# A long convolution and a gated MLP on one core: where the last inverse stage's copy, sum and difference stand in the queues

## The chip, the cores and the metric

The kernel runs on one core of a Trainium2 chip. The metric is the device time of one execution in microseconds (us). The engines are called as the profile calls them: PE (TensorE, matrix products, with PEld for its weight loads), DVE (VectorE), ACT (ScalarE), POOL (GpSimd) and SP (SyncE, which here issues every DMA). Each engine works through its own instructions in the order in which they are written, and waits at an instruction until the others have delivered.

## The reference

Two layers follow each other. The first convolves `x*v` along the sequence (4 batches, 12480 positions, 128 channels) with a filter that a small network makes, and multiplies by `x`; the second is a gated MLP with 2048 inner features.

```python
h_filt = (np.maximum(pos_emb @ w1, 0.0) @ w2) * np.exp(-0.01 * pos)[:, None]
u = x * v
y = irfft(rfft(u, 2*S) * rfft(h_filt, 2*S), 2*S)[:, :S]   # along the sequence
x1 = (x * y).reshape(B * S, D)
h = x1 @ w_in
out = (h * np.clip(h + 3.0, 0.0, 6.0) / 6.0) @ w_out
```

## The kernel before, in words

The transforms are done as two short transforms each, as products with tables on PE. The convolution is cut into eight groups of channels and batches (`NG = 8`), each group into 25 chunks (`NCHUNK`) of four frequencies. The function `period(g)` walks through the chunks of group g and writes, chunk by chunk, work of three groups side by side:

- of group g itself (`chunk`): PE makes the chunk's spectra (`second_stage`, L300). ACT copies their two halves crosswise into another PSUM bank, the swap (`swapped`, L498 and L499; there is one such bank, tag `sw`). DVE multiplies spectra and swapped spectra with the filter's (`products`, L519 to L522). POOL adds the products up in three steps (L526): two small additions, into `a` and into `a2`, and the final sum `a + a2`. Three chunks later PE takes the sum back (`third_stage`, L541) and ACT copies the result into `z` (L545).
- of group g - 1, whose `z` is complete: PE transposes it (`back`, L552), ACT copies the transposes into `w` (L555), and for every fourth of these (one block of 16 columns) the last inverse stage follows (`fourth_stage`): PE multiplies the block with a table into two PSUM banks, `same` and `other` (L569), ACT copies `other` into SBUF (L579), DVE forms sum and difference of `same` and this copy (L581, two instructions), and SP stores the block to `yd` in HBM (L584).
- of group g + 1: POOL multiplies loaded pieces of `x` and `v` (`gate_next`, L452, eight or nine for a group), and eight times for a group PE makes a first stage of four tiles (`visit`, L281), each copied into `z` by ACT (L293).

During the first group, which has no group ahead of it to take back, DVE does the final sum of two chunks in three (L531; chunks whose number is not a multiple of 3), and POOL does the others.

The first stages, `back` and the fourth stage share one set of three PSUM banks (tag `ts`); a new tile takes the bank that was let go first. The spectra share two banks (tag `s2`). In the first groups of those that have a `back`, DVE also decodes the MLP's weights in small steps (L225 to L247), in three stretches for each of five groups and one more.

After the eighth group `last_turn` takes its own `z` back, and then the MLP (class `Moe`) runs for the rest of the time. Nothing is reordered by a scheduler: the order in the code is the order in each engine's queue.

Of the kernel before, what the change touches and what calls it, by code (L numbers as in the profile page):

```python
# [188 lines left out]
def pool(tc, name, bufs=1, **kw):  # L189
    return tc.tile_pool(name=name, bufs=bufs, reuse_waits="tile", **kw)  # L190
# [60 lines left out]
class Conv:  # L251
    def __init__(self, tc, nc, left, right, x, v, c_tab, d_tab, g_tab, ident, hd, yd, weights):
        self.tc, self.nc, self.left, self.right = tc, nc, left, right
        self.x, self.v, self.g_tab, self.ident, self.hd, self.yd = x, v, g_tab, ident, hd, yd
        self.c_tab, self.d_tab, self.weights = c_tab, d_tab, weights
        self.loaded, self.gated, self.n_loaded = [], [], 0
        self.first, self.second, self.pend, self.steps = [], [], [], None
        self.tabs, self.n_tabs, self.hs, self.n_hs = [], 0, [], 0
        self.keep = right.enter_context(pool(tc, "keep", side="right"))
        self.z = [self.keep.tile([128, K2, COLS], F32, name=f"z{i}") for i in range(2)]  # L260
        self.dtab = self.keep.tile([K2, 2, 64], F32, name="dtab")
        big = left.enter_context(pool(tc, "big"))
        self.ctab = big.tile([R[0], 2 * K2], F32, name="ctab")
# [238 lines left out]
    def products(self, item):  # L502

        nc, P = self.nc, 128
        g, c, kw, t, tab = item
        sw = self.swapped(t, kw)
        hs = self.hs.pop(0)
        a = self.pr.tile([P, CH, 2 * GB, G], F32, tag="a", name="pa", bufs=4)
        a2 = self.pr.tile([P, CH, 2 * GB, G], F32, tag="a2", name="pa2")
        q = self.pr.tile([P, CH, GB, G], F32, tag="q", name="pq")  # L510
        q2 = self.pr.tile([P, CH, GB, G], F32, tag="q2", name="pq2")
        uv = t.rearrange("p (k s g) -> p k s g", k=CH, g=G)[:, :kw]
        sv = sw.rearrange("p (k s g) -> p k s g", k=CH, g=G)[:, :kw]

        def h(ci, si, m):
            return hs[:, ci, :kw, si, :].unsqueeze(2).to_broadcast([P, kw, m, G])

        mul, add = ALU.mult, ALU.add
        nc.vector.tensor_tensor(out=q[:, :kw], in0=uv[:, :, :GB], in1=h(0, 1, GB), op=mul)  # L519
        nc.vector.tensor_tensor(out=a[:, :kw], in0=uv, in1=h(0, 0, 2 * GB), op=mul)  # L520
        nc.vector.tensor_tensor(out=q2[:, :kw], in0=sv[:, :, :GB], in1=h(1, 1, GB), op=mul)
        nc.vector.tensor_tensor(out=a2[:, :kw], in0=sv, in1=h(1, 0, 2 * GB), op=mul)  # L522
        self.load_h()

        def plus(x, y):
            nc.gpsimd.tensor_tensor(out=x, in0=x, in1=y, op=add)  # L526

        plus(a[:, :kw, GB:], q[:, :kw])
        plus(a2[:, :kw, GB:], q2[:, :kw])
        if g == 0 and c % 3:  # L530
            nc.vector.tensor_tensor(out=a[:, :kw], in0=a[:, :kw], in1=a2[:, :kw], op=add)  # L531
        else:
            plus(a[:, :kw], a2[:, :kw])
        return g, c, kw, tab, a
# [24 lines left out]
    def fourth_stage(self):  # L559


        if not self.pend:
            return
        nc = self.nc
        g, col, w = self.pend.pop(0)
        same, other = (self.bank("ts") for i in range(2))
        for c, t in enumerate((same, other)):
            for h in range(2):
                nc.tensor.matmul(  # L569
                    t[64 * h : 64 * h + 64, :],  # L570
                    self.dtab[:, c, :],
                    w[:, GH * h : GH * h + GH, c * N1 : (c + 1) * N1],
                    start=True,
                    stop=True,
                )
        y = self.wp.tile([128, 2, N1, GH], F32, tag="y", name="y")
        same, other = (t.rearrange("p (c n) -> p n c", c=GH) for t in (same, other))
        o = self.wp.tile([128, N1, GH], F32, tag="o", name="o", bufs=1)
        nc.scalar.copy(o, other)  # L579
        for i, op in enumerate((ALU.add, ALU.subtract)):  # L580
            nc.vector.tensor_tensor(out=y[:, i], in0=same, in1=o, op=op)  # L581
        piece, ch = divmod(col, G)
        k, b, d = self.place(g, piece)
        nc.sync.dma_start(self.yd[b][k][d // G, ch // GY], y)  # L584
# [29 lines left out]
    def chunk(self, g, c):  # L614

        if g == 0 and c == 0:
            self.first.append(self.spectra(0, 0))
        self.second.append(self.products(self.first.pop(0)))
        lag = LAG if START < c < NCHUNK - 1 else LAG - 1
        self.third_from(lag)  # L620
        g, c = (g, c + 1) if c + 1 < NCHUNK else (g + 1, 0)
        if g < NG:
            self.first.append(self.spectra(g, c))
        self.third_from(lag)
# [26 lines left out]
    def last_turn(self, moe):  # L651

        self.fourth_stage()
        for n, col in enumerate(range(0, COLS, 4)):
            self.back(NG - 1, col)
            if n % 4 == 2:
                self.fourth_stage()
            if n in (10, 12):
                moe.load(n // 2 - 5)
            if n == 20:  # L660
                moe.gate(0)
            if n == 28:
                moe.turn(0)
        self.fourth_stage()


class Moe:
# [208 lines left out]
```

## Time and profile before

| | |
|---|---|
| median of three runs | 3205.4 us (3201.54 to 3206.84) |
| profiled execution, its own time | 3204.68 us |
| its span in the profile | 3202.9 us |
| PE busy | 3125.8 us (98%) |
| DVE busy | 2328.0 us (73%) |
| ACT busy | 2347.2 us (73%) |
| POOL busy | 2078.4 us (65%) |
| PE's granted clock, mean over the span | 0.997 of 2.4 GHz |

The span runs from the first to the last instruction on the engines; 1.8 us of the execution's own time lie around it. The ends of PE's products are modelled, so that a busy PE can still be short of its peak; its idle time is the safer figure. A matrix product of 32-bit numbers shows as two records.

### The profile page before, as it was taken

To read this page: it belongs to the slowest core of one execution; us is meant where nothing else is said; L and a number is where in the kernel's file an instruction comes from. 1 tells how busy PE (TensorE), PEld (TensorE's weight loads), DVE (VectorE), ACT (ScalarE), POOL (GpSimd) and SP (SyncE) were. 2 spreads that over 40 slices of the span, in tenths; PEclk is the share of its full clock that TensorE was granted. 3 is DMA by queue.
4 is the path that set the end of the run, shared out by engine and by line. 5 is a ranking of instruction groups with operands and counts; after the bars stand their busy time and mean duration, and the time that the engine had idled before them with its cause. 6 is when DMAs were issued, how large, how long until landed. Compare 5 with 4: busy or idle time off the path is not lost.

```text
span 3202.9 us, 53380 instructions
## 1 busy us (share of the span) xinstructions
PE 3125.8 (98%) x19916; PEld 2638.1 (82%) x19916; DVE 2328.0 (73%) x2707; ACT 2347.2 (73%) x3039; POOL 2078.4 (65%) x1240
## 2 busy tenths in 40 slices
PE   9978999999999999999999999999999999999999
PEld 8967888888887788888888888888888888888887
DVE  4467677667656577777777777777777777777776
ACT  2346676666677787787777777777777877778777
POOL 1167777777777366666666666666666666666666
PEclk9999999999999999999999999999999999999999
DMA  6667878877765311111111111011011111111110
GB/s 230 211 167 201 238 217 225 226 216 229 215 183 187 117 30 40 40 33 41 33 40 37 33 40 40 30 40 40 30 40 40 30 40 40 33 37 40 36 35 23
DMA packets 232273, 304.66 MB, mean 95 GB/s; under 512 B 38055, under 2 KB 159310, under 8 KB 231118
## 3 DMA queue, kind: packets, MB, share of 16 engines
q1 hardware_dynamic: 232014, 301.26, 32.2%
q8 instruction: 157, 2.57, 0.3%
q14 instruction: 102, 0.84, 0.1%
HBM read 224.87 MB, written 76.28 MB: 94 GB/s over the span
## 4 chain that ended last, share of the span: by engine, by line
PE 67%; POOL 0%; DVE 0%; DMA 0%; ACT 0%; issue 0%; ACTq 0%
PE acc L808 11%; PE acc L804 11%; PE acc L805 11%; PE ph L769 11%; PE ph L771 11%; PE ph L770 11%; PE ts L569 1%; PE s L552 0%; PE ts L552 0%; POOL pa L526 0%; DMA yd<-y 0%; POOL glo L793 0%; DVE y L581 0%; ACT ghi L791 0%; PE s L541 0%; DVE o L821 0%
## 5 line engine op out<-in xcount | busy, mean ns | idle before, releaser
L793 POOL TENSOR_TENSOR glo<-g,ghi 128x1024 fp32r<-128x1024 f32 x588 | 1405.6, 2399 | 759.3 <-ACT ghi L791 759.2
L781 DVE SCALAR_TENSOR_TENSOR g<-r,ph 128x1024 f32<-128x1024 f32 (+1 forms) x784 | 949.5, 1211 | 408.5 <-ACT r L779 408.3
L779 ACT ACTIVATE r<-ph,three 128x1024 f32<-128x1024 f32 (+1 forms) x784 | 871.3, 1111 | 273.7 <-PE ph L771 273.4
L791 ACT CAST ghi<-g 128x1024 fp32r<-128x1024 f32 (+1 forms) x784 | 810.9, 1034 | 1.9 <-DVE g L781 1.0
L769 PE MATMUL ph<-xhi,win_hi 128*128 128x512 f32 (+1 forms) x1568 | 608.5, 388 | 0.0
L770 PE MATMUL ph<-xlo,win_hi 128*128 128x512 f32 (+1 forms) x1568 | 608.4, 388 | 0.0
L771 PE MATMUL ph<-xhi,win_lo 128*128 128x512 f32 (+1 forms) x1568 | 608.3, 388 | 0.0
L805 PE MATMUL acc<-ghi,wout_lo 128*128 128x512 f32 (+1 forms) x1568 | 608.0, 388 | 0.0
L804 PE MATMUL acc<-ghi,wout_hi 128*128 128x512 f32 (+1 forms) x1568 | 607.9, 388 | 0.0
L808 PE MATMUL acc<-glo,wout_hi 128*128 128x512 f32 (+1 forms) x1568 | 481.3, 388 | 0.6 <-POOL glo L793 0.6
L526 POOL TENSOR_TENSOR pa<-pa,pq 128x256 f32<-128x256 f32 (+1 forms) x400 | 291.5, 735 | 209.1 <-DVE pa L520 175.8
L769 PEld LDWEIGHTS ph<-xhi,win_hi 128*128 128x128 f32 x1568 | 294.5, 188 | 61.6 <-issue 0.8
L808 PEld LDWEIGHTS acc<-glo,wout_hi 128*128 128x128 f32 x1568 | 293.5, 188 | 61.9 <-POOL glo L793 1.5
L805 PEld LDWEIGHTS acc<-ghi,wout_lo 128*128 128x128 f32 x1568 | 294.5, 188 | 60.6
L770 PEld LDWEIGHTS ph<-xlo,win_hi 128*128 128x128 f32 x1568 | 294.5, 188 | 60.3
L771 PEld LDWEIGHTS ph<-xhi,win_lo 128*128 128x128 f32 x1568 | 294.3, 188 | 60.6
L804 PEld LDWEIGHTS acc<-ghi,wout_hi 128*128 128x128 f32 x1568 | 294.3, 188 | 60.4
L793 DVE TENSOR_TENSOR glo<-g,ghi 128x1024 fp32r<-128x1024 f32 x196 | 284.2, 1450 | 0.0
L300 PE MATMUL s<-z,tab 128*128 128x128 f32 x1584 | 218.7, 282 | 57.9 <-DVE pa L520 28.3
L742 DVE TENSOR_TENSOR xy<-xt,yt 128x512 f32<-128x512 f32 x96 | 258.5, 2693 | 0.0
L300 PEld LDWEIGHTS s<-z,tab 128*128 128x128 f32 x1584 | 195.3, 194 | 69.3 <-issue 29.4
L526 POOL TENSOR_TENSOR pa<-pa,pa 128x512 f32<-128x512 f32 (+1 forms) x184 | 233.6, 1270 | 14.4
(61 smaller groups left out, 3529.6 us busy)
## 6 DMA issues: line engine op xcount, KB each, us to landing
tab<-in_g_tab SPq DMA_DIRECT2D x192, 256.0 KB
h<-hd SPq DMA_DIRECT2D x384, 128.0 KB
yd<-y SPq DMA_DIRECT2D x64, 512.0 KB
xt<-in_xt SPq DMA_DIRECT2D x98, 256.0 KB
out<-o SPq DMA_DIRECT2D x97, 256.0 KB
xt<-in_x SPq DMA_DIRECT2D x64, 384.0 KB
vt<-in_v SPq DMA_DIRECT2D x64, 384.0 KB
yt<-yd SPq DMA_DIRECT2D x256, 64.0 KB
```

The lines of the kernel that those rows point to most:

```text
L300: self.nc.tensor.matmul(t[:, i * 128 : (i + 1) * 128], tab[:, i, :], z[:, c * CH + i, :], start=True, stop=True)
L526: nc.gpsimd.tensor_tensor(out=x, in0=x, in1=y, op=add)
L769: nc.tensor.matmul(ph[:, i, :ne], self.win_hi[:, sl], hi[:, :ne], start=True, stop=False)
L770: nc.tensor.matmul(ph[:, i, :ne], self.win_hi[:, sl], lo[:, :ne], start=False, stop=False)
L771: nc.tensor.matmul(ph[:, i, :ne], self.win_lo[:, sl], hi[:, :ne], start=False, stop=True)
L779: nc.scalar.activation(r[:, :, :ne], ph[:, :, :ne], AF.Relu, bias=self.three)
L781: nc.vector.scalar_tensor_tensor(out=g[:, :, :ne], in0=r[:, :, :ne], scalar=6.0, in1=ph[:, :, :ne], op0=ALU.min, op1=ALU.mult)
L791: nc.scalar.copy(ghi[:, :, :ne], g[:, :, :ne])
L793: e.tensor_tensor(out=glo[:, :, :ne], in0=g[:, :, :ne], in1=ghi[:, :, :ne].bitcast(F32), op=ALU.subtract)
L804: nc.tensor.matmul(a, self.wout_hi[:, f, :], ghi[:, i, :ne], start=(f == 0), stop=False)
L805: nc.tensor.matmul(a, self.wout_lo[:, f, :], ghi[:, i, :ne], start=False, stop=False)
L808: nc.tensor.matmul(a, self.wout_hi[:, f, :], glo[:, i, :ne], start=False, stop=(f == NFC - 1))
```

## The change

`fourth_stage` is cut in two. It keeps the products on PE, and remembers their two banks; the copy on ACT, the sum and the difference on DVE and the store move into a new function, `results`, which is called behind the next chunk's `products` (or, where a second block would come first, ahead of that block's products on PE). In `last_turn` it is called right behind each fourth stage. And in the first group the final sum that DVE does for a chunk is written one chunk later, behind that chunk's four multiplications.

```diff
+        if self.sum:
+            s, s2 = self.sum
+            nc.vector.tensor_tensor(out=s, in0=s, in1=s2, op=add)
+        self.sum = None
         if g == 0 and c % 3:
-            nc.vector.tensor_tensor(out=a[:, :kw], in0=a[:, :kw], in1=a2[:, :kw], op=add)
+            self.sum = a[:, :kw], a2[:, :kw]
         else:
             plus(a[:, :kw], a2[:, :kw])
...
         if not self.pend:
             return
+        self.results()
         nc = self.nc
         g, col, w = self.pend.pop(0)
...
+        self.out = g, col, same, other
+
+    def results(self):
+
+        if self.out is None:
+            return
+        nc = self.nc
+        g, col, same, other = self.out
+        self.out = None
         y = self.wp.tile([128, 2, N1, GH], F32, tag="y", name="y")
...
         self.second.append(self.products(self.first.pop(0)))
+        self.results()
         lag = LAG if START < c < NCHUNK - 1 else LAG - 1
...
         self.fourth_stage()
+        self.results()
```

No instruction is added or removed. With the two insertions the lines move: what is L498, L499, L519 to L522, L531, L579 and L581 before is L499, L500, L520 to L523, L533, L594 and L596 after.

On DVE in the first group, at the products of chunks 4, 5 and 6 (`pa` is a chunk's `a`, `pa2` its `a2`, `s2` its spectra, `sw` the swap), before:

```order
L522 TENSOR_TENSOR pa2_2148<-sw_2144,h_2004 128x512
L531 TENSOR_TENSOR pa_2147<-pa_2147,pa2_2148 128x512
L519 TENSOR_TENSOR pq_2186<-s2_2169,h_2033 128x256
L520 TENSOR_TENSOR pa_2184<-s2_2169,h_2033 128x512
L521 TENSOR_TENSOR pq2_2187<-sw_2181,h_2033 128x256
L522 TENSOR_TENSOR pa2_2185<-sw_2181,h_2033 128x512
L531 TENSOR_TENSOR pa_2184<-pa_2184,pa2_2185 128x512
L519 TENSOR_TENSOR pq_2216<-s2_2206,h_2055 128x256
```

The same place on DVE after the change:

```order
L523 TENSOR_TENSOR pa2_2148<-sw_2144,h_2004 128x512
L520 TENSOR_TENSOR pq_2185<-s2_2168,h_2033 128x256
L521 TENSOR_TENSOR pa_2183<-s2_2168,h_2033 128x512
L522 TENSOR_TENSOR pq2_2186<-sw_2180,h_2033 128x256
L523 TENSOR_TENSOR pa2_2184<-sw_2180,h_2033 128x512
L533 TENSOR_TENSOR pa_2147<-pa_2147,pa2_2148 128x512
L520 TENSOR_TENSOR pq_2215<-s2_2205,h_2054 128x256
L521 TENSOR_TENSOR pa_2213<-s2_2205,h_2054 128x512
L522 TENSOR_TENSOR pq2_2216<-sw_2210,h_2054 128x256
L523 TENSOR_TENSOR pa2_2214<-sw_2210,h_2054 128x512
L533 TENSOR_TENSOR pa_2183<-pa_2183,pa2_2184 128x512
```

The sum of chunk 4 (`pa_2147`) stood directly behind its own products and now stands behind those of chunk 5; that of chunk 5 stands behind those of chunk 6.

On ACT in the third group (group 2, which takes group 1 back), behind the visit and fourth stage of chunk 3 (`z1` copies are the visit's, `sw` the swap of chunk 4, `o` the copy of `other`), before:

```order
L293 COPY z1_79<-ts_4772 128x99x4
L579 COPY o_4789<-ts_4783 128x512
L498 COPY sw_4794<-s2_4725 64x512
L499 ACTIVATE sw_4794<-s2_4725 64x512
L545 COPY z0_78<-s3_4811 128x512
```

The same place on ACT after the change:

```order
L294 COPY z1_79<-ts_4772 128x99x4
L499 COPY sw_4788<-s2_4725 64x512
L500 ACTIVATE sw_4788<-s2_4725 64x512
L594 COPY o_4806<-ts_4783 128x512
L550 COPY z0_78<-s3_4811 128x512
```

The swap of chunk 4 now stands ahead of the fourth stage's copy; on DVE sum and difference likewise stand behind the products of chunk 4.

On DVE in the same group, behind the products of chunk 18 and at the first steps of the third weight decoding (`dec`), before:

```order
L581 TENSOR_TENSOR y_5694<-ts_5688,o_5695 128x512 x2
L519 TENSOR_TENSOR pq_5712<-s2_5637,h_5444 128x256
L520 TENSOR_TENSOR pa_5710<-s2_5637,h_5444 128x512
L521 TENSOR_TENSOR pq2_5713<-sw_5707,h_5444 128x256
L522 TENSOR_TENSOR pa2_5711<-sw_5707,h_5444 128x512
L225 TENSOR_SCALAR dec_5562<-raw_5560 128x256
```

The same place on DVE after the change:

```order
L520 TENSOR_TENSOR pq_5706<-s2_5637,h_5444 128x256
L521 TENSOR_TENSOR pa_5704<-s2_5637,h_5444 128x512
L522 TENSOR_TENSOR pq2_5707<-sw_5701,h_5444 128x256
L523 TENSOR_TENSOR pa2_5705<-sw_5701,h_5444 128x512
L596 TENSOR_TENSOR y_5718<-ts_5688,o_5719 128x512 x2
L225 TENSOR_SCALAR dec_5562<-raw_5560 128x256
```

Sum and difference of that block now stand between the products of chunk 19 and the decoding. On PE and POOL the order of the instructions is the same in both kernels.

## Rows read from the trace of the kernel before

**Rows 1.** Busy time by stretch: stretch, length, PE, PEld, DVE, ACT, POOL, clock, DMA.

```profile
164.00:265.00 101.00, 77.09 (x886) 71.12 (x886) 73.23 (x112) 51.85 (x102) 65.88 (x65) 0.93 0.69 181
265.00:1034.00 769.00, 728.72 (x7189) 633.38 (x7190) 525.16 (x992) 531.68 (x1016) 585.34 (x574) 1.00 0.75 213
1076.00:3202.00 2126.00, 2121.91 (x9403) 1757.70 (x9401) 1641.21 (x1370) 1686.60 (x1763) 1405.65 (x588) 1.00 0.12 37
```

**Rows 2.** Timeline of DVE, first group: start, length, instruction, [idle before it, what ended it].

```profile
210.56 0.69 DVE L531 TENSOR_TENSOR pa<-pa,pa 128x512 f32<-128x512 f32 x1 [0.84 <-POOL pa L526]
211.17 0.42 DVE L519 TENSOR_TENSOR pq<-s,h 128x256 f32<-128x256 f32 x1
...
212.44 0.68 DVE L522 TENSOR_TENSOR pa<-sw,h 128x512 f32<-128x512 f32 x1
213.96 2.83 DVE L531 TENSOR_TENSOR pa<-pa,pa 128x512 f32<-128x512 f32 x1 [0.84 <-POOL pa L526]
216.71 0.41 DVE L519 TENSOR_TENSOR pq<-s,h 128x256 f32<-128x256 f32 x1
...
219.93 0.42 DVE L519 TENSOR_TENSOR pq<-s,h 128x256 f32<-128x256 f32 x1 [1.28 <-ACT sw L499]
...
223.33 0.42 DVE L519 TENSOR_TENSOR pq<-s,h 128x256 f32<-128x256 f32 x1
```

**Rows 3.** Timeline of POOL, the same stretch.

```profile
213.88 2.36 POOL L452 TENSOR_TENSOR u<-xt,vt 98x1024 f32<-98x1024 f32 x1
...
218.79 0.72 POOL L526 TENSOR_TENSOR pa<-pa,pq 128x256 f32<-128x256 f32 x1 [0.19 <-DVE pa L522]
```

**Rows 4.** All of line 531: durations in ns (least, median, most), first and last start.

```profile
L531 DVE TENSOR_TENSOR pa<-pa,pa x16: 692/1754/2849, 171.8 to 264.8; 128x512 f32<-128x512 f32 x16
```

**Rows 5.** Timeline of ACT, the same stretch of the first group.

```profile
216.49 0.49 ACT L293 COPY z<-ts 128x396 f32<-128x396 f32 x1 [0.19 <-PE ts L281]
218.74 0.56 ACT L498 COPY sw<-s 64x512 f32<-64x512 f32 x1 [1.75 <-DVE pa L522]
```

**Rows 6.** Timeline of the third group, chunks 3 to 5, around a fourth stage.

```profile
394.46 1.90 PE L569 MATMUL ts<-w,dtab 99*64 99x512 f32 x8
...
394.68 0.49 ACT L293 COPY z<-ts 128x396 f32<-128x396 f32 x1 [0.19 <-PE ts L281]
...
396.39 0.59 ACT L579 COPY o<-ts 128x512 f32<-128x512 f32 x1 [1.23 <-PE ts L569]
...
397.01 1.29 DVE L581 TENSOR_TENSOR y<-ts,o 128x512 f32<-128x512 f32 x2 [3.78 <-ACT o L579]
...
398.25 0.42 DVE L519 TENSOR_TENSOR pq<-s,h 128x256 f32<-128x256 f32 x1
...
399.05 0.59 ACT L555 COPY w<-ts 99x512 f32<-99x512 f32 x1 [0.38 <-PE ts L552]
...
400.29 0.56 ACT L498 COPY sw<-s 64x512 f32<-64x512 f32 x1 [0.65 <-DVE pa L522]
```

**Rows 7.** Timeline of the third group, chunks 12 to 14, with a decoding.

```profile
434.75 1.91 PE L569 MATMUL ts<-w,dtab 99*64 99x512 f32 x8
...
436.70 0.59 ACT L579 COPY o<-ts 128x512 f32<-128x512 f32 x1 [1.23 <-PE ts L569]
...
438.48 1.52 PE L552 MATMUL ts<-ident,z 128*99 128x128 f32 x8
```

**Rows 8.** Timeline of the third group, chunks 18 to 20, with a decoding.

```profile
465.11 1.29 DVE L581 TENSOR_TENSOR y<-ts,o 128x512 f32<-128x512 f32 x2 [3.11 <-ACT o L579]
...
469.10 0.28 DVE L225 TENSOR_SCALAR dec<-raw 128x256 int32<-128x256 int32 x1
...
470.52 0.42 DVE L519 TENSOR_TENSOR pq<-s,h 128x256 f32<-128x256 f32 x1 [0.18 <-issue]
```

**Rows 9.** Waits of PE, 265 to 1034 us: total us, times, longest.

```profile
PE s L300 <- DVE pa L520: 16.7, 20, 1.8
...
PE ts L552 <- ACT z L545: 4.3, 7, 1.3
```

More of the change, by code (lines that the diff above doesn't have):

```diff
@@ L258, in __init__ @@
         self.tabs, self.n_tabs, self.hs, self.n_hs = [], 0, [], 0
+        self.out, self.sum = None, None
         self.keep = right.enter_context(pool(tc, "keep", side="right"))
@@ L657, in last_turn @@
                 self.fourth_stage()
+                self.results()
             if n in (10, 12):
@@ L664, in last_turn @@
         self.fourth_stage()
+        self.results()
 class Moe:
```

## The prediction

> **What bounds the kernel now.** I read the busy time by stretch first, because the change touches only the convolution [rows 1]. The MLP, from 1076 us on, has PE busy for 2121.91 of 2126.00 us, and the change leaves its order alone, so I count nothing there. Groups 1 to 7 (265 to 1034 us) are nearly the same case: PE is idle for 769.00 - 728.72 = 40.3 us, and that is the most that any change of waits can return. The first group (164 to 265 us) is another: PE has 77.09 us of work in 101.00, and no engine is full. Something in its order sets the pace, and the place to look is the chain from one chunk to the next.
>
> The timeline of DVE shows that chain [rows 2]. Between the first multiplications of successive chunks lie 216.71 - 211.17 = 5.54 us, 219.93 - 216.71 = 3.22 us and 223.33 - 219.93 = 3.40 us; then it repeats, 12.16 us for three chunks. The middle one holds no sum. It is four multiplications (213.12 - 211.17 = 1.95 us) and 1.28 us in which DVE waits for the swap, which in turn waits for the fourth multiplication [rows 2, 5], as there is one swap bank. The other two hold a final sum. It first waits 0.84 us for POOL's small addition, and takes 0.69 us in the one case and 2.83 in the other. The long one started at 213.96, just behind POOL's `gate_next`, which ran from 213.88 to 216.24 [rows 3]; the sum was over at 216.79. So it stood still until POOL was done and then took its own 0.6. Over all of the 16 sums the least is 692 ns and the most 2849, with a middle value of 1754 between two equal halves [rows 4]: 8 of each.
>
> **The change: the sum of the first group.** One chunk later the sum stands behind the next chunk's four multiplications, where DVE has 1.28 us to wait for the swap in any case. Its inputs are long there, so the 0.84 goes, and 0.69 fits in 1.28. If every chunk took the 3.22 us of the one without a sum, three would take 9.66 in place of 12.16, and eight such triples 20.0 us less; that is the upper bound of this term. PE would allow it: its 77.09 us of work in the group are less than the 101.00 - 20.0 that remain.
>
> Two things stand against the full 20. First the visit: ACT copies its four tiles in the same queue as the swaps. The last of them started at 216.49, 5.32 us behind the triple's first multiplication at 211.17, and ended at 5.81 [rows 5]; it had waited 0.19 us for PE, so that it is PE's order that places it. With a cycle of 3.22 the next swap could start at 3.22 + 1.95 + 0.1 = 5.27, and stands behind that copy for about 0.5 us. Eight visits make 4.0. Second, the gate itself is still there, 2.36 us long. It starts as before behind the second small addition of its chunk, some 2.7 us after that chunk's first multiplication, or up to 3.4 if the moved sum holds POOL back by its 0.69; it ends 5.1 to 5.8 after. A moved sum that is ready at 3.22 + 1.95 = 5.17 stands still until then and has its 0.6 done by 6.4. The next chunk's multiplications come at 2 x 3.22 + 0.5 = 6.9, so the gate no longer reaches the chain. Only if the gate ended more than 0.5 us later than this would it. The term is -20.0 + 4.0 = **-16.0 us**, with -20 and 0 as its ends.
>
> The trace shows both orders of a collision: the sum of 213.96 began 0.08 us behind the gate and stood for 2.3 us, and the sum of 210.56, beside no gate, ran in 0.69. The Trainium skill ("SBUF — State Buffer", "Who interferes with whom") says that DVE and GpSimd share one pair of ports as a lock held for a whole instruction, and that a DVE instruction with two SBUF inputs contends with a GpSimd instruction that reads SBUF; that half of the sums agrees with this is the 2.83 against 0.69. By that rule the moved sum has a new neighbour, since it starts in the moment in which POOL starts its second small addition: 1.95 + 0.72 + 0.69 = 3.36 instead of 3.22, 0.14 us on each of 16 sums, and the whole sum would come out 2.2 us higher. I do not add it: it lies inside the range.
>
> **The change: copy, sum and difference.** In 64 fourth stages nothing is added; some 52 have their copy, sum, difference and store behind the next products. In the third group, chunks 3 to 5, the copy began at 396.39, and ACT had waited for it 1.23 us, for the products that ran from 394.46 to 396.36; the swap of chunk 4, ready long before, stood behind it [rows 6]. Now the swap (two instructions, about 1.15 us) takes that 1.23, and the copy comes at the same time as before. The 128x512 bank is released for PE no later, which is why I expect no new wait of PE on these banks. The products of chunk 4 run from 396.4 to 398.35, not from 398.25 to 400.2. Sum and difference follow to 399.65. The swap of chunk 5 is then held by `back`'s copy, 399.05 + 0.59 = 399.64, where it started at 400.29: 0.65 us earlier. On PE's path that counts only where PE waits for DVE or ACT soon behind it.
>
> PE's waits in groups 1 to 7 give the sizes [rows 9]. At a group's first `back` PE waits for the last `z`, 4.3 us in 7 times, at most 1.3. The copy of 0.59 us ahead of that `z` on ACT goes behind it: I take -3.0, between nothing and -4.3. Spectra that wait for DVE stand for 16.7 us in 20 times, at most 1.8. These lie in the weight decodings, where DVE is the engine waited for. At chunks 12 to 14 the copy stays at 436.70, before the second `back` at 438.48 could need a bank [rows 7]; the sums move behind the products there, and up to 1.8 us can come back: I take half, -0.9. At chunks 18 to 20 it goes the other way: sum and difference ran at 465.11, behind 3.11 us of idle DVE, which hid them, and now stand between the products and the first decoding step of 469.10, with the next multiplications at 470.52 behind 0.18 us only [rows 8]. The cover is gone, and I take the whole 1.29 as lost. Five groups with decodings make 5 x (-0.65 - 0.9 + 1.29) = -1.3, the two others -0.65 each. In `last_turn` the results of the block before come behind the last `z`; the copy and the pair are at most 0.59 + 1.29 = 1.88, of which I take 0.7. The stores on SP go 2 us later, ahead of nothing that is waited for. The term is -3.0 - 1.3 - 1.3 + 0.7 = **-4.9 us**; its ends are -40.3, all of PE's idle time, and 5 x 1.29 + 1.88 = +8.3.
>
> **Sum.** 3204.68 - 16.0 - 4.9 = 3183.8 us, so 3184. The profiled execution is 0.7 us under the median of 3205.4, which changes nothing.
>
> **Rivals.** (a) The decodings cost and nothing comes back in groups 1 to 7: +8.3 in place of -4.9, so 3197; for it speaks the full DVE of [rows 8], against it the waits of [rows 9] that are shorter with an earlier swap. (b) With earlier swaps most of the idle time of groups 1 to 7 goes, half of 40.3: 3169; against it speaks that only 16.7 + 4.3 = 21.0 of it waits for what the change moves. (c) The change does not do what it says in the first group: the moved sum is held by the gate until behind the next swap, each visit loses the same 2.3 us a chunk later, the 0.18 of a short sum returns at most. Then 3204.68 - 1.4 - 1 is about 3202, no change; it decides where the gate ends later than 6.9 - 0.6 = 6.3 us behind the triple's start. (d) Slower: the sums read the two banks of the fourth stage, and end 399.65 instead of 398.30, 1.35 us later. If PE's next tile in this set needs `same` and not `other`, PE stands at each of the 52. With half of the 1.35 each that is +35, and 3204.68 - 16.0 + 35 is about 3224; at 0.3 us each it eats up the first term. Against it speaks that the bank let go first is `other`, by the copy.
>
> **How the numbers follow.** The forecast has 0.58, (a) 0.17, (b) 0.09, (c) 0.10, (d) 0.06. A measurement of this kernel tells about 0.2%, 6.4 us, from no change: the forecast, (a) and (b) are faster, 0.84, (c) the same, 0.10, and (d) slower, 0.06. The range goes from 3166, under (b), to 3198, above (a), and leaves out (c) and (d).
>
> **What would show it.** In the changed profile all 16 moved sums (L533) should last 0.69, or up to 1.4 beside a small addition, and few be over 2; the starts of L520 should lie 3.2, 3.7 and 3.2 us apart, and the first group end near 249 instead of 265. The copy (L594) should have no 1.23 us of idle time before it, and L596 should follow the products. The decodings of chunks 19 to 22 should run 1.3 us later against their group's start. The MLP should last 2126. The forecast is wrong if PE waits for a `ts` bank on L594 or L596, or if the long sums have only changed their place.

## The result, and the profile after

The changed kernel takes 3167.8 us (median of five runs, 3166.5 to 3171.2) where the kernel before takes 3205.4: 0.9886 of its time, 95% interval 0.9872 to 0.9901, 37.6 us less. The forecast was 3184, 21.4 us less, so the direction was right and the gain nearly twice the forecast; the time lies in the range, near its lower end.

In the profiled executions the span falls from 3202.9 to 3164.7 us, by 38.2. The two traces can be laid over each other instruction by instruction, since PE's order is the same. Worked from the starts of single instructions in both timelines:

```
                                              before     after    earlier by
first multiplication, first group (chunk 0)   164.01    161.01       3.00
first multiplication, second group            268.19    246.28      21.91
last fourth stage's products                 1071.91   1033.73      38.18
end                                          3202.9    3164.7       38.2
```

So the first group gives 18.9 us, groups 1 to 7 with the last turn 16.3, and the MLP nothing. The first 3.0 us are not the change's: they are there ahead of everything that it touches. PE's timeline of the first microseconds shows it, before the change

```profile
5.11 2.95 PE L339 MATMUL h<-z,w1bd 128*128 128x392 f32 x4 [5.11 <-DMA z<-in_pos_emb]
8.57 12.23 PE L339 MATMUL h<-z,w1bd 128*128 128x392 f32 x28 [0.51 <-DMA z<-in_pos_emb]
20.64 14.14 PE L356 MATMUL h<-w2bd,ht 128*98 128x128 f32 x128
```

and after:

```profile
5.14 12.65 PE L340 MATMUL h<-z,w1bd 128*128 128x392 f32 x32 [5.14 <-DMA z<-in_pos_emb]
17.64 14.14 PE L357 MATMUL h<-w2bd,ht 128*98 128x128 f32 x128
```

Before the change these 32 products were held up once more by a load, and then ran slower. In the twelve profiled executions of this study (experiments too) chunk 0's first multiplication starts anywhere from 161.0 to 166.2 us, whatever the kernel. Below, gains in a trace are therefore counted from that point on: 35.2 us for the change.

**The first group** takes 85.3 us from its first multiplication to the second group's, not 104.2. By stretch, before and after (columns as in [rows 1]):

```profile
164.00:268.20 104.20, 79.22 (x902) 72.98 (x902) 75.15 (x117) 53.96 (x106) 67.55 (x68) 0.93 0.70 183
```

```profile
161.00:246.30 85.30, 72.61 (x894) 68.19 (x895) 60.45 (x117) 53.69 (x105) 72.43 (x68) 0.98 0.90 216
```

PE's idle time halves, 25.0 to 12.7 us, and POOL is now busy for 72.4 of 85.3 us. DVE's timeline over three chunks, which answers to [rows 2]:

```profile
215.91 0.42 DVE L520 TENSOR_TENSOR pq<-s,h 128x256 f32<-128x256 f32 x1 [1.02 <-ACT sw L500]
...
219.17 0.42 DVE L520 TENSOR_TENSOR pq<-s,h 128x256 f32<-128x256 f32 x1 [1.30 <-ACT sw L500]
...
221.03 0.68 DVE L533 TENSOR_TENSOR pa<-pa,pa 128x512 f32<-128x512 f32 x1
222.42 0.42 DVE L520 TENSOR_TENSOR pq<-s,h 128x256 f32<-128x256 f32 x1 [0.70 <-ACT sw L500]
...
224.29 0.90 DVE L533 TENSOR_TENSOR pa<-pa,pa 128x512 f32<-128x512 f32 x1
226.21 0.42 DVE L520 TENSOR_TENSOR pq<-s,h 128x256 f32<-128x256 f32 x1 [1.02 <-ACT sw L500]
```

The distances are 3.26, 3.25 and 3.79 us: 10.30 for three chunks instead of 12.16. Both sums now lie in the time that DVE waits for the swap. POOL and ACT in the same stretch, which answer to [rows 3] and [rows 5]:

```profile
222.26 2.37 POOL L453 TENSOR_TENSOR u<-xt,vt 98x1024 f32<-98x1024 f32 x1
224.59 1.86 POOL L527 TENSOR_TENSOR pa<-pa,pq 128x256 f32<-128x256 f32 x2
```

```profile
214.21 0.49 ACT L294 COPY z<-ts 128x396 f32<-128x396 f32 x1 [0.19 <-PE ts L282]
214.72 0.56 ACT L499 COPY sw<-s 64x512 f32<-64x512 f32 x1
```

The gate ends at 224.63, 5.46 us behind the first multiplication at 219.17; the sum that meets it stands for some 0.2 us, is over at 225.19, and the next multiplication comes at 226.21. The swap at 214.72 stands right behind the visit's last copy. All 16 sums, which answer to [rows 4]:

```profile
L533 DVE TENSOR_TENSOR pa<-pa,pa x16: 676/704/1916, 169.4 to 244.6; 128x512 f32<-128x512 f32 x16
```

**Groups 1 to 7.** In the third group, chunks 3 to 5, ACT and DVE (in this order) now show what answers to [rows 6]:

```profile
371.05 0.56 ACT L499 COPY sw<-s 64x512 f32<-64x512 f32 x1
371.64 0.57 ACT L500 ACTIVATE sw<-s 64x512 f32<-64x512 f32 x1
372.26 0.59 ACT L594 COPY o<-ts 128x512 f32<-128x512 f32 x1
...
374.92 0.59 ACT L560 COPY w<-ts 99x512 f32<-99x512 f32 x1 [0.98 <-PE ts L557]
375.53 0.56 ACT L499 COPY sw<-s 64x512 f32<-64x512 f32 x1
```

```profile
372.30 0.42 DVE L520 TENSOR_TENSOR pq<-s,h 128x256 f32<-128x256 f32 x1 [3.22 <-issue]
...
374.17 1.28 DVE L596 TENSOR_TENSOR y<-ts,o 128x512 f32<-128x512 f32 x2
376.78 0.42 DVE L520 TENSOR_TENSOR pq<-s,h 128x256 f32<-128x256 f32 x1 [1.33 <-POOL pa L527]
```

The copy's 1.23 us of idle time are gone, since the swap fills them. From this fourth stage's start (370.31; 394.46 before) to the next swap it takes 5.22 us, not 5.83. PE's waits, 246 to 1034 us, which answer to [rows 9]:

```profile
PE s L301 <- DVE pa L521: 15.7, 13, 2.1
PE s L301 <- issue: 2.8, 2, 1.4
...
PE ts L557 <- ACT z L550: 1.0, 1, 1.0
...
PE ts L557 <- DVE y L596: 0.2, 1, 0.2
```

The `ts` banks are waited for on sum and difference once, for 0.2 us. Laid over each other at the starts of fourth stages, the kernels part in nearly the same steps in each middle group; those of the third:

```
from one fourth stage's start to the next         earlier by
chunk 0 to chunk 3 (380.86 to 394.46 before)         0.86
to the next (408.01), with chunk 5                   0.61
to the next (421.87), first decoding                 0.88
chunk 12 to chunk 15, second decoding (449.62)       1.27
chunk 18 to chunk 24, third decoding (490.32)       -1.43
```

With two steps under 0.1 left out this is 2.2 us for the group. The sixth group alone has 2.62 at its second decoding. The 1.35 us on top belong to the one execution before the change: PE's granted clock there was 0.81 (782.00 to 791.15 us), and in `gate_fill` and `gate_twice_before` below, which have the old order in these groups, that step is 1.35 us shorter and another group's 1.4 to 1.5 longer.

### The profile page after: what moved, and what is told of

The parts are those of the page before. It is cut to its first block, busy times and chain, and to the rows that moved or that the text cites. A ratio compares the mean times of both kernels' runs of the same rounds, so it can differ in the third digit from the quotient of the medians.

```text
span 3164.7 us, 53332 instructions
## 1 busy us (share of the span) xinstructions
PE 3114.2 (98%) x19916; PEld 2633.9 (83%) x19916; DVE 2305.8 (73%) x2707; ACT 2351.7 (74%) x3039; POOL 2079.2 (66%) x1240
## 4 chain that ended last, share of the span: by engine, by line
PE 68%; POOL 0%; DVE 0%; ACT 0%; DMA 0%; issue 0%; ACTq 0%
PE acc L827 11%; PE acc L823 11%; PE acc L824 11%; PE ph L788 11%; PE ph L790 11%; PE ph L789 11%; PE ts L575 0%; PE s L557 0%; PE ts L557 0%; POOL pa L527 0%; DMA yd<-y 0%; POOL glo L812 0%; DVE y L596 0%; ACT o L594 0%; ACT ghi L810 0%
## 5 line engine op out<-in xcount | busy, mean ns | idle before, releaser
L520 DVE TENSOR_TENSOR pq<-s,h 128x256 f32<-128x256 f32 (+1 forms) x200 | 84.1, 421 | 255.7 <-POOL pa L527 162.2
```

## The experiments

All are timed in five rounds against the kernel before on the same chip.

**The two parts alone.** `sum_only` is the kernel before with

```diff
+        if self.sum:
+            s, s2 = self.sum
+            nc.vector.tensor_tensor(out=s, in0=s, in1=s2, op=add)
+        self.sum = None
         if g == 0 and c % 3:
-            nc.vector.tensor_tensor(out=a[:, :kw], in0=a[:, :kw], in1=a2[:, :kw], op=add)
+            self.sum = a[:, :kw], a2[:, :kw]
```

and `results_only` the changed kernel without these lines, so that DVE's sum stands at its old place.

> Only the first group's final sum stands one chunk later; copy, sum and difference of the last stage stand as before. Theory: the two parts act in different groups and add up; the trace after the change has the first group's part at 18.9 us (the second group begins 21.9 us earlier, 3.0 of which are there before the first visit already), so 3205.4 - 19 = about 3186.5, with the second group to the eighth as long as before. Rival: the sum moves only a wait, and the products' freedom from the copy is what shortens the first group's end and all that follows; then this kernel gains under 8 us, above 3197.

> Only copy, sum, difference and store stand behind the next chunk's products; the first group's final sum stands as before. Theory: groups 1 to 7 with the last turn gain 16.3 us as in the trace after the change, the first group nothing: 3205.4 - 16.3 = about 3189. My own term of the prediction for this part was -4.9, which would give 3200.5. Rival: the gain of groups 1 to 7 needs the first group to have been shortened (other phase of the transfers); then about 3201 to 3205.

`sum_only` takes 3184.6 us against 3205.9 (0.9938, 0.9925 to 0.9950), `results_only` 3188.0 (0.9945, 0.9932 to 0.9957). In the traces, counted from chunk 0, the first gains 19.0 us in the first group and loses 1.2 behind it; the second gains 0.3 in the first group and 16.6 behind it. The parts add up: 21.2 + 17.9 = 39.1 against 37.6. Both rivals fall.

**What the long sums stood for.** `gate_fill` is the kernel before with

```diff
+            if self.filling:
+                self.nc.gpsimd.memset(u, 0.0)
+                self.nc.gpsimd.tensor_tensor(out=u[:, :1, :1], in0=xt[:, :1, :1], in1=vt[:, :1, :1], op=ALU.mult)
+            else:
+                self.nc.gpsimd.tensor_tensor(out=u, in0=xt, in1=vt, op=ALU.mult)
```

> The kernel before the change, with the nine gate multiplications of the first group's chunks replaced by a fill of the same tile with zeros (and a product of one element a partition, which keeps the waits for the loaded pieces); it leaves the products x*v of these pieces out. Theory: the long sums (2.83 us instead of 0.69) stand still because the gate on POOL reads SBUF for its whole length while the sum reads two tiles there; a fill reads nothing, so all 16 sums last 0.69 us and 8 x 2.1 = 17 us are gained, about 3188. Rival: the sum waits because POOL is busy with anything as long (a wait of order, not of what is read); then the long sums remain as long as the fill lasts, and the gain is 8 times whatever the fill is shorter than the gate.

It takes 3186.1 us (0.9938, 0.9926 to 0.9951), and the first group is 16.5 us shorter in the trace. All sums are short, though eight of them still start about 0.1 us behind a fill. One of the fills, and all sums:

```profile
206.39 0.95 POOL L454 MEMSET u<- 98x1024 f32 x1
```

```profile
L536 DVE TENSOR_TENSOR pa<-pa,pa x16: 691/692/694, 170.8 to 248.2; 128x512 f32<-128x512 f32 x16
```

The sum of 206.48 started 0.09 us behind a fill of 0.95 us and took its 0.69. The rival would have it stand until 207.34, and last some 1.5. So what holds the sum is not that POOL is busy; the gate reads SBUF, and the fill doesn't. The Trainium skill ("SBUF — State Buffer", "Who interferes with whom") says the same of a GpSimd instruction that only writes: it does not contend with a two-input DVE instruction.

`gate_fill_after` is the same edit in the changed kernel.

> The changed kernel with the first group's gates replaced by the fill (it leaves the products x*v of these pieces out). Theory: in the changed kernel the sum's meeting with the gate costs the chain nothing any more (0.90 instead of 0.69 us at most places, inside DVE's wait for the swap), so a gate that reads nothing changes nothing: 3165 to 3169. Rival: part of the lock still lies on the chain, or POOL's time does; then up to 8 x 0.5 = 4 us and more are gained, under 3164.

3170.4 us (0.9894, 0.9881 to 0.9908), and 18.8 us gained in the first group as against 18.9. What is left of the lock costs the chain nothing that shows.

**Longer gates.** `gate_twice_before` and `gate_twice_after` do each of these multiplications twice:

```diff
             self.nc.gpsimd.tensor_tensor(out=u, in0=xt, in1=vt, op=ALU.mult)
+            if self.filling:
+                self.nc.gpsimd.tensor_tensor(out=u, in0=xt, in1=vt, op=ALU.mult)
```

> The kernel before the change with the same doubled gates. Theory: the sum behind a gate stands until the gate's end and the next products behind it, so all of the added time is paid: 8 x 2.4 = 19 us, about 3224.5, and the long sums last 5.2 us. Rival: POOL's small additions give the pace; then less, under 3215.

> The changed kernel with each gate multiplication of the first group's chunks done twice (same inputs, same output), so that POOL is held 2.4 us longer at eight or nine places. Theory: the gate still holds the moved sum, but the sum is not in the products' way for about 1.0 us behind the gate's end (sum over at 6.0, next multiplication at 7.0 us behind its triple's second chunk in the trace after); 8 x (2.4 - 1.0) = 11 us lost, about 3179. Rival 1: the moved sum is free of the gate altogether; no loss, about 3168. Rival 2: no cover at all, each longer gate is paid in full, 8 x 2.4 = 19: about 3187.

Before: 3209.5 us against 3205.8 (1.0016, 1.0007 to 1.0025), +3.7 where I expected +19 (in the trace the first group is 5.4 us longer). POOL and DVE there:

```profile
218.99 2.36 POOL L453 TENSOR_TENSOR u<-xt,vt 98x1024 f32<-98x1024 f32 x1
221.43 2.69 POOL L455 TENSOR_TENSOR u<-xt,vt 98x1024 f32<-98x1024 f32 x1
```

```profile
219.06 2.83 DVE L534 TENSOR_TENSOR pa<-pa,pa 128x512 f32<-128x512 f32 x1 [0.84 <-POOL pa L529]
```

The sum still takes 2.83: it goes when the first gate ends, and the second gate stands for it, 2.69 instead of 2.36. The experiment did not double the wait that I meant to double. After: 3186.0 us (0.9939, 0.9926 to 0.9951), 18.3 more than the changed kernel's 3167.8; in the traces 14.9 of it lie in the first group and 2.4 behind. That is near rival 2's number, but not for its reason. The first group's stretch there, and PE's longest waits from 160 to 270 us:

```profile
164.50:264.70 100.20, 79.48 (x886) 74.14 (x886) 68.17 (x117) 54.63 (x105) 92.21 (x76) 0.89 0.75 180
```

```profile
PE s L549 <- POOL pa L530: 6.7, 4, 2.8
PE s L549 <- DVE pa L536: 5.7, 3, 3.6
```

POOL is busy for 92.2 of 100.2 us, and PE waits for the sums themselves; PE's granted clock was lower too, 0.89 where the kernel after has 0.98. So POOL bounds this kernel. That it is the next bound of the kernel after, where it is busy for 72.4 of 85.3 us, is likely but not shown, and the margin of about 1 us that I wanted to measure stays unmeasured, except that it is there (225.19 against 226.21 above).

**Which of the two places counts in groups 1 to 7.** `copy_at_once` takes the copy alone back to the fourth stage:

```diff
+        o = self.wp.tile([128, N1, GH], F32, tag="o", name="o", bufs=1)
+        nc.scalar.copy(o, other.rearrange("p (c n) -> p n c", c=GH))
-        self.out = g, col, same, other
+        self.out = g, col, same, o
```

> The changed kernel, but ACT copies `other` at its old place, directly behind the products of the fourth stage; only sum, difference and store stand behind the next chunk's products. Theory: what gains in groups 1 to 7 is that the swap stands ahead of the copy on ACT; with the copy back at its place the next swap waits again for the fourth stage, its 1.15 us are no longer covered by sum and difference (1.29 us) on DVE, the products come at most 0.15 us earlier than before the change, and the decodings lose their 1.3 to 1.4 us in five groups: the first group's 19 us remain and 0 to 7 us are lost, 3186 to 3194. Rival: it is the place of sum and difference on DVE that gains; then about 3168 to 3172.

`pair_behind_swap` puts sum and difference back ahead of the products, with the copy behind the swap:

```diff
         sw = self.swapped(t, kw)
+        self.results()
...
         self.second.append(self.products(self.first.pop(0)))
-        self.results()
```

> The changed kernel, but copy, sum, difference and store stand between the next chunk's swap and its four multiplications: on ACT the swap is ahead of the copy as in the changed kernel, on DVE sum and difference are ahead of the products as before the change. Theory: both places are needed; here the products wait for the copy by way of sum and difference, and come at the same time as before the change (398.25 in the third group), so that groups 1 to 7 gain only the 0.5 us of each boundary: 3205.6 - 19 - 3 = about 3183 to 3187. Rival: the swap's place on ACT alone brings the gain; then 3166 to 3171.

They take 3212.8 us (1.0022, 1.0013 to 1.0031) and 3211.9 (1.0024, 1.0015 to 1.0033, against 3204.7). With the first group's gain in both (18.1 from chunk 0), groups 1 to 7 with the last turn are 26.5 and 23.4 us longer than before the change: each half of the move, as written here, is worse than none, and my prices were wrong.

Laid over the kernel before, `copy_at_once` loses 8.5 us at the third decodings, where the pair stands as in the changed kernel, 5.8 at the second (with the sixth group's 1.35 us taken off) and 3.0 at the first ones; and 8.6 at six group boundaries, where two fourth stages stand close together. There the second copy waits 2.82 us, six times, because `o` has one buffer (`bufs=1`) and the first block's sum and difference still read it:

```profile
491.12 0.59 ACT L583 COPY o<-ts 128x512 f32<-128x512 f32 x1 [2.82 <-DVE y L596]
```

This third of the loss goes with the one buffer; no run gives `o` a second one, so that it is not shown what the place alone costs there. At the second decoding of the fourth group no such wait stands in the way. DVE there, then ACT:

```profile
547.18 0.42 DVE L520 TENSOR_TENSOR pq<-s,h 128x256 f32<-128x256 f32 x1 [1.54 <-POOL pa L527]
...
549.05 1.28 DVE L596 TENSOR_TENSOR y<-ts,o 128x512 f32<-128x512 f32 x2
...
553.15 0.42 DVE L520 TENSOR_TENSOR pq<-s,h 128x256 f32<-128x256 f32 x1
```

```profile
545.33 0.59 ACT L583 COPY o<-ts 128x512 f32<-128x512 f32 x1 [1.23 <-PE ts L575]
545.94 0.56 ACT L499 COPY sw<-s 64x512 f32<-64x512 f32 x1
```

Before the change sum and difference ran while ACT made the swap. Here DVE idles through copy and swap, and pays the 1.28 us behind the products. The products of 553.15 come 9.77 us behind the fourth stage's start; it was 9.08 before the change and is 7.95 in the changed kernel. PE's step there is 0.54 us longer than before. It is 1.9 to 2.1 us longer in the three groups in which the granted clock fell as well (0.91 over 20 us).

Where the pair stands between swap and products it is in the chain itself; this is DVE at the third decoding of the fourth group:

```profile
568.75 1.29 DVE L597 TENSOR_TENSOR y<-ts,o 128x512 f32<-128x512 f32 x2 [5.67 <-ACT o L595]
569.95 0.41 DVE L521 TENSOR_TENSOR pq<-s,h 128x256 f32<-128x256 f32 x1
```

The swap was done at 568.21; the products come 1.7 us later, and PE's step there is 1.7 us longer. Before the change the pair ran there in a time that DVE had nothing else to do. I had looked only at blocks like that of chunk 3, where the old place was late already.

**How long the banks may be held.** `behind_z` moves the call of `results` in `chunk` from behind `products` to the function's end.

> The changed kernel with copy, sum, difference and store placed still later, behind the chunk's z copies on ACT, so that the two banks of a fourth stage are held 0.6 to 1.7 us longer. Theory: the banks have room, since the second back that could need one starts some 3.6 us behind the copy (chunk 4 of the fourth group); no change beyond 4 us either way, 3164 to 3172. Rival, the prediction's slower case: each such delay of a bank is waited for by PE at the 52 moved places; 0.6 us each would be +31, about 3199.

3171.5 us (0.9896, 0.9882 to 0.9909): in the trace 33.6 us from chunk 0, against 35.2. PE waits for a `ts` bank on sum and difference still only once, 0.2 us. The banks have room, and rival (d) is gone.

**The step that goes the other way.** `block24_at_once`:

```diff
                         self.fourth_stage()
+                        if n == 24 and 0 < g < 6:
+                            self.results()
```

> The changed kernel, but in groups 1 to 5 copy, sum, difference and store of the block whose fourth stage lies just ahead of the third decoding (chunk 18) follow the fourth stage at once, as before the change; all others stand as in the changed kernel. Theory: there the moved pair fell out of an idle DVE into the decoding, which cost 1.4 us in each of these groups (PE's step at this place is +1.4 in all five); taken back it gives 5 x 1.4 = 7 us: 3167.8 - 7 = about 3161. Rival: the pair is needed behind the products there too, since the swap then waits for the copy again; then no change, 3166 to 3170.

3162.4 us (0.9866, 0.9851 to 0.9881), the fastest of all, 5.4 under the changed kernel, though the intervals of the two ratios overlap. Laid over the kernel before, the step of -1.4 at the third decoding is gone in all five groups (0.0 each); that settles the cause of this step. The profiled execution is with 3166.3 the slowest of the four, and loses 3.9 us at the start of the second group, which this edit doesn't reach: PE waited 2.08 us there for the load of a table. At the third decoding of the third group DVE now does the pair in its old idle time, well ahead of the decoding:

```profile
443.47 1.29 DVE L596 TENSOR_TENSOR y<-ts,o 128x512 f32<-128x512 f32 x2 [3.06 <-ACT o L594]
445.59 0.42 DVE L520 TENSOR_TENSOR pq<-s,h 128x256 f32<-128x256 f32 x1 [0.83 <-issue]
```

PE's wait for spectra on DVE, 16.7 us before the change and still 15.7 after it, shows here (249.22 to 1033.46 us) as

```profile
PE s L301 <- DVE pa L521: 7.1, 10, 1.1
```

So in the changed kernel the third decodings had taken back, in this wait, most of what the other places had given.

## Why the prediction was right in direction and short in size

**The first group: -16.0 forecast, -18.9 in the trace.** The mechanism held, and its numbers came close: sums in DVE's wait for the swap, 10.16 us for three chunks forecast and 10.30 measured, the gate over 5.1 to 5.8 us behind its chunk and 5.46 measured, the next products at 6.9 and 7.04. What I mis-sized is the start of the group. I counted eight equal triples; but from chunk 1 to chunk 8 the gain is 7.7 us in seven chunks, not 4.7. Four of these seven distances were long before the change (5.17, 5.52, 5.53 and 5.21 us), where [rows 2] has one in three. Two held a long sum, behind the gates of chunks 2 and 4. In one a swap stood behind a visit's copies, which ACT made late, waiting for PE. And in one even a short sum had waited 2.61 us for POOL, which did the gate of chunk 0 first:

```profile
171.83 0.69 DVE L531 TENSOR_TENSOR pa<-pa,pa 128x512 f32<-128x512 f32 x1 [2.61 <-POOL pa L526]
```

The new neighbour of the sum, which the prediction weighed at 0.14 us a chunk, costs the chain nothing that shows: a chunk with the sum takes 3.25 us, one without 3.26. It is POOL's pair of additions that stands: 1.97 us for the two beside the sum of 221.03, where two took 1.59 before the change (at 212.33, with no sum beside them).

**Groups 1 to 7: -4.9 forecast, -16.3 in the trace.** This is the failing term, by its size. Added up over all groups from the steps between fourth stages, the term's parts are (in us, minus is a gain):

```
                                       forecast   measured
boundary, third to seventh group         -3.0       -4.3
earlier swap ahead of chunk 5            -4.55      -3.9, and -1.9 in the eighth group
first decoding, six groups               none       -5.3
second decoding, five groups             -4.5       -7.7 (1.35 of it the lower clock before)
third decoding, five groups              +6.45      +7.1
last turn                                +0.7       +0.6
steps under 0.4                          none       -0.9
```

(The forecast's -3.0 counts seven boundaries.) The third decoding's loss and the last turn's were right, and so was the earlier swap's 0.65 (0.61 in the third group). What failed first is the part that has no term: the prediction looked at the second decoding and the third, but not at the first. There too sum and difference stood ahead of the next products in a busy DVE before the change:

```profile
411.51 1.28 DVE L581 TENSOR_TENSOR y<-ts,o 128x512 f32<-128x512 f32 x2
412.71 0.41 DVE L519 TENSOR_TENSOR pq<-s,h 128x256 f32<-128x256 f32 x1
```

Moved behind the products they gave 0.88. Second, two waits were halved, and came back nearly whole. The second decoding gave 1.27 of a wait of 1.75 where I took 0.9. The group's boundary gave 0.86 in place of 0.43: the wait for `z` shows as 0.51 of it, and the rest lies in PE's products right before and behind it, whose starts stand further apart than without the wait. The forecast also put all of the spectra's 16.7 us into the decodings; in the third group 0.45 of it stands ahead of the first one, at chunk 5, and that is the wait which the earlier swap ended. Third group: 0.69 forecast, 2.2 measured.

**The rivals.** (b) has the measured time almost to the microsecond (3169 against 3167.8), and that is partly luck: its 20.2 us for groups 1 to 7 measured 16.3, its 16.0 for the first group 18.9, and 3.0 us of the profiles' difference are not the change's. Its mechanism, PE's waits behind the earlier swaps going as well, is what the trace shows in part. From the second group's first multiplication to the last fourth stage, before and after:

```profile
268.19:1071.91 803.72, 764.50 (x7363) 657.56 (x7363) 534.27 (x1005) 553.08 (x1052) 583.68 (x572) 1.00 0.74 214
```

```profile
246.28:1033.73 787.45, 762.09 (x7373) 658.83 (x7371) 526.98 (x1005) 557.88 (x1052) 580.87 (x572) 0.99 0.76 219
```

PE's idle time falls from 39.2 to 25.4 us, by a third and not by half. I gave (b) 0.09 because I read only the waits whose releaser the change moves, 21.0 us. (a) was true of the third decoding, which does cost what it says; the first and the second gained. (c) and (d) do not occur.

**Left open.** Why the profiled execution of the changed kernel had the earliest start of twelve; what `copy_at_once` would take with a second buffer for `o`; and why PE's granted clock falls in one group of an execution and not in another. That also stands behind the 1.2 us which `sum_only` loses behind the first group: its third group's second decoding takes 1.55 us longer, at a clock of 0.81 (421 to 430 us).

## What to carry to other kernels

A piece of work that must go somewhere in an engine's queue costs nothing in the place where the engine waits for the others anyway, and its whole length in the chain; look for that place on each engine that the piece uses, and move the whole chain of it, as half a move can be worse than none (here in part for want of a second buffer). Where such a piece had an idle time of its own already (the block ahead of the third decoding), leave it there: one rule for all places gave away 1.4 us in each of five groups. When a wait on a chain recurs, count its places in the whole trace, and ask which waits behind it fall with it, before taking a half.

## What the runs showed of the hardware

A two-input addition of 128x512 on DVE stood 2.1 us behind a POOL multiplication that reads SBUF, and not at all beside a POOL fill of 0.95 us, which reads nothing. When two POOL multiplications stood in a row, the waiting addition went between them (2.83 us, as with one), and the second took 2.69 us instead of 2.36; the collision's price did not grow with POOL's queue.
